# A planned kernel learns that GpSimd and VectorE exclude each other on SBUF operands

## The chip, the cores and the metric

One core of a Trainium2 chip runs the whole program. The metric is the device time of one execution in microseconds (us). A core has five engines that work side by side, each through its own instructions in a fixed order, and they meet at semaphores: TensorE (PE, matmuls), VectorE (DVE), ScalarE (ACT), GpSimd (POOL), and SyncE (SP), which issues the DMAs here. Matmuls write to PSUM; DVE and ACT read PSUM and SBUF; in this kernel POOL works on SBUF alone.

## The reference

```
# x: 8 x 8 heads x 512 x 64, state: 8 x 8 heads x 32 x 64
scores  = x @ state^T / 8 ;  xread = softmax(scores) @ state      # 512 rows a head
scores2 = state @ x^T / 8 ;  sread = softmax(scores2) @ x         # 32 rows a head
y   = concat([xread, sread]) -> (8*544) x 512
y   = ((y @ w_a) * (y @ w_b)) @ w_out                  # moe,  512 -> 1536 -> 512
out = (silu(y @ w_gate) * (y @ w_val)) @ w_out2        # moe2, 512 -> 1536 -> 512
```

The inputs x and state are fp32, the weights arrive as 64-bit floating point numbers and are converted in the kernel.

## The kernel before, in words

**Precision.** A matmul operand is held as two fp32r halves, hi and lo, and a product takes three matmuls (hi*hi, hi*lo, lo*hi). `split` and `hi_lo` (L317, L324) make the halves: ACT casts to hi, then one subtraction on DVE or POOL makes lo. There are hundreds of these subtractions; unless the source lies in PSUM, the planner may put each on DVE or on POOL (`dve_pool`).

**Weights.** `convert` (L345 to L377) turns 64-bit numbers to fp32: two ACT passes, a clamp (DVE or POOL, L363), a shift and a merge (DVE, L368 and L371), and an integer addition that only POOL does (L375). This addition occurs 72 times. `second_weights` (L689 on) makes sums and differences of converted weights on DVE (L700), splits them and sends them to DRAM.

**Attention.** `quad`, `softmax1` and `softmax2` (L479 to L632) do four heads at a time. Softmax uses 32x32 transposes and grouped reductions on DVE, an exponential on ACT, and two broadcasts (L533, L548) on DVE or POOL.

**First moe.** For each of eight blocks of 512 tokens and one of 256 state rows, `moe` (L650 to L686) multiplies by twelve weight columns a and b (L645), ACT or DVE copies a out of PSUM, DVE multiplies by b from PSUM (L664), the product is split (tile hs), and four output products (L680) add up in PSUM. Tile names ending in _s are those of the state block.

**Second moe.** `operands` and `second` (L719 to L817) handle two blocks at a time by a scheme of seven products for eight. Sums of the inputs are made on DVE (L738), fourteen splits (tile x) feed the products (L750), and DVE combines results in PSUM (L764, L771). `unit` (L844) makes the output products, `finish` (L862) adds and stores.

**The planner.** `Program` (L103 to L240) fixes the order of the work. Each call of `add` makes a task with the engines that may do it, a modelled cost on each, what it reads and writes, and a due time `by`. `order` plays a simulation of the five queues: whenever an engine is free, it takes the ready task with the earliest due time for which there is buffer room. A task that two engines may do is left for the other engine where that one would finish it sooner by the model. The outcome is an engine for each task and an order of instructions on each engine; nothing of the modelled times is enforced on the chip, where semaphores alone hold the engines. The modelled costs are L62: DVE 0.07 us and 1.05 ns a column, or 0.53 ns for fast forms, POOL 0.2 us and 2.6 ns a column. So a subtraction of 512 columns is counted as 0.61 us on DVE and 1.53 us on POOL. `HOP_US` (L64) is the modelled delay from the end of a task to the start of one that waits for it. In the model of before, DVE and POOL run independently of each other.

Of the kernel before, what the change touches and what calls it, by code (L numbers as in the profile page):

```python
# [10 lines left out]
F32 = mybir.dt.float32  # L11
# [4 lines left out]
ALU = mybir.AluOpType  # L16
AX = mybir.AxisListType

P = 128
# [40 lines left out]
ROOM = {"w": 44, "h": 20, "pt": 2}  # L60

ACT_US, DVE_US, FAST_US, POOL_US = ((0.09, 0.84e-3), (0.07, 1.05e-3), (0.07, 0.53e-3), (0.2, 2.6e-3))  # L62
PASS_US, HALF_PASS_US = 0.2267, 0.12
HOP_US, PE_HOP_US = 0.15, 0.3  # L64
DMA_US, DMA_ISSUE_US, DMA_BYTES_PER_US = 2.2, 0.5, 3.6e5

DMA_AHEAD_US = 1

# [14 lines left out]
class Buf:  # L83


    def __init__(self, tag, name, make, after=None):
        self.tag, self.name, self.make, self.after = tag, name, make, after
        self.t = None
        self.parts = {}
        self.tasks = set()  # L90


class Task:
    def __init__(self, i, engines, fn, bufs, deps, by, start, size):
# [4 lines left out]
        self.new = []  # L99
        self.engine, self.main = None, 0.0  # L100


class Program:  # L103

# [4 lines left out]
        self.tasks = []  # L109
        self.first = 0.0  # L110

    def add(self, engines, fn, r=(), w=(), by=1e9, start=0.0, size=0):
        deps, bufs = set(), []
        for x, writes in [(x, False) for x in r] + [(x, True) for x in w]:
            b, part = x if isinstance(x, tuple) else (x, None)
            assert writes or b.tasks, "read before anything wrote it"
            if writes and b.after is not None:
                deps |= b.after.tasks
            for p, (last, readers) in b.parts.items():
                if part is None or p is None or p == part:  # L120
                    if last is not None:
                        deps.add(last)
                    if writes:
                        deps |= readers
            bufs.append((b, part, writes))
        t = Task(len(self.tasks), engines, fn, list(dict.fromkeys(b for b, _, _ in bufs)), deps, by, start, size)
        t.deps.discard(t)
        for b, part, writes in bufs:
            if writes:
                if part is None:  # L130
                    b.parts = {}
                b.parts[part] = (t, set())
            else:
                for p in [p for p in b.parts if part is None or p is None or p == part]:
                    b.parts[p][1].add(t)
            b.tasks.add(t)
        self.tasks.append(t)
        return t

    def order(self):  # L140
        tasks = self.tasks
        for t in tasks:
            for d in t.deps:
                d.next.append(t)
        for t in reversed(tasks):
            for n in t.next:
                t.by = min(t.by, n.by - n.cost - HOP_US - (DMA_US + n.size / DMA_BYTES_PER_US if n.size else 0))
        room = dict(ROOM)
        left = {b: len(b.tasks) for t in tasks for b in t.bufs}
        made = set()  # L150
        waits = {t: len(t.deps) for t in tasks}
        when = dict.fromkeys(tasks, 0.0)
        gates = sorted((t for t in tasks if t.start), key=lambda t: -t.start)
        main = 0.0
        ready = {e: [] for e in ("PE", "ACT", "DVE", "POOL", "DMA")}
        free = dict.fromkeys(ready, 0.0)
        wire = 0.0
        events = []

        def offer(t):  # L160
            heapq.heappush(events, (when[t], 0, t.i, t))

        for t in tasks:
            waits[t] += t.start > 0
            if not waits[t]:
                offer(t)
        now, done = 0.0, []
        while events:
            now = events[0][0]
            main = max(main, min(now, self.first))  # L170
            while gates and gates[-1].start <= main:
                t = gates.pop()
                waits[t] -= 1
                when[t] = max(when[t], now)
                if not waits[t]:
                    offer(t)
            while events and events[0][0] <= now + 1e-9:
                _, kind, _, t = heapq.heappop(events)
                if kind == 0:
                    for e in t.engines:  # L180
                        heapq.heappush(ready[e], (t.by, t.i, t))
                elif kind == 1:
                    for b in t.bufs:
                        left[b] -= 1
                        if not left[b] and b.tag in room:
                            room[b.tag] += 1
            for e, heap in ready.items():
                if free[e] > now + 1e-9:
                    continue
                held = []  # L190
                while heap:
                    item = heapq.heappop(heap)
                    t = item[2]
                    if t.engine is not None:
                        continue
                    t.new = [b for b in t.bufs if b not in made]
                    need = {}
                    for b in t.new:
                        if b.tag in room:
                            need[b.tag] = need.get(b.tag, 0) + 1  # L200
                    if any(room[k] < n + (RESERVE[k] if t.by > main + FAR_US else 0) for k, n in need.items()) or any(
                        max(free[o], now) + sum(q[2].engines[o] for q in ready[o] if q < item and q[2].engine is None)
                        + c < now + t.engines[e] - (SPARE_US if e != "DVE" and t.by > main + 5 else 0) - 1e-9
                        for o, c in t.engines.items() if o != e
                    ):
                        held.append(item)
                        continue
                    for k, n in need.items():
                        room[k] -= n
                    made.update(t.new)  # L210
                    t.engine, t.at = e, now
                    us = t.engines[e] * (2.0 if e == "PE" and t.engines[e] < 1.0 and main <= self.first else 1.0)
                    free[e] = end = now + us
                    main = max(main, t.main)
                    if e == "DMA":
                        wire = max(wire, now) + t.size / DMA_BYTES_PER_US
                        end = max(wire, end) + DMA_US
                        free[e] = max(free[e], wire - DMA_AHEAD_US)
                    heapq.heappush(events, (free[e], 2, t.i, t))
                    heapq.heappush(events, (end, 1, t.i, t))  # L220
                    for n in t.next:
                        waits[n] -= 1
                        hop = HOP_US if e != "PE" else 0.0 if "PE" in n.engines else PE_HOP_US
                        when[n] = max(when[n], end + hop)
                        if not waits[n]:
                            offer(n)
                    done.append(t)
                    break
                for item in held:
                    heapq.heappush(heap, item)  # L230
        self.end = now
        assert len(done) == len(tasks), f"{len(tasks) - len(done)} tasks found no room, at {now:.0f} us"
        return done
# [8 lines left out]
class Kernel:  # L242
# [32 lines left out]
    def bank(self, name, out=None):  # L275

        if out is not None:
            return self.ring(f"po{out}", 1, name, self.ps)
        return Buf("pt", name, lambda: self.ps.tile([P, 512], F32, tag="pt", bufs=ROOM["pt"], name=name))

    def dram(self, name, shape, dtype=F32):
        return Buf(None, name, lambda: self.dr.tile(shape, dtype, tag=name, name=name))
# [1 line left out]
    def ring(self, tag, n, name, pool=None, dtype=F32, shape=(512,)):  # L284

        old = self.rings.setdefault(tag, [])
        pool = pool or self.sb
        b = Buf(
            None, name, lambda: pool.tile([P, *shape], dtype, tag=tag, bufs=n, name=name),
            old[-n] if len(old) >= n else None,  # L290
        )
        old.append(b)
        return b

# [226 lines left out]
    def softmax1(self, b, g, sT, by):  # L521
# [3 lines left out]
        sn = self.h_buf(f"sn{nm}")  # L525
        mx, sm = (self.ring(k, 2, f"{k}{nm}", shape=(16, 1)) for k in ("mx", "sm"))
        grouped = lambda t: t.rearrange("p (a n) -> p a n", n=NS)
        kw = {"by": by}
        self.vec(512, lambda v: v.transpose(sn.t, sT.t), [sT], [sn], **kw)
        self.vec(  # L530
            512, lambda v: v.tensor_reduce(mx.t[:, :, 0], grouped(sn.t), axis=AX.X, op=ALU.max), [sn], [mx], **kw
        )
        self.p.add(dve_pool(512), lambda e: self.by_engine[e].tensor_tensor(  # L533
            out=grouped(sn.t), in0=grouped(sn.t), in1=mx.t.to_broadcast([P, 16, NS]), op=ALU.subtract
# [2 lines left out]
            act(512), lambda e: nc.scalar.activation(out=sn.t, in_=sn.t, func=AF.Exp, scale=SCALE), [], [sn], **kw  # L537
        )
        self.vec(
            512, lambda v: v.tensor_reduce(sm.t[:, :, 0], grouped(sn.t), axis=AX.X, op=ALU.add), [sn], [sm], **kw  # L540
        )

        def rest(v):
# [5 lines left out]
            out=grouped(sn.t), in0=grouped(sn.t), in1=sm.t.to_broadcast([P, 16, NS]), op=ALU.mult  # L549
        ), [sm], [sn], **kw)  # L550
        at = self.h_buf(f"at{nm}")
        self.vec(512, lambda v: v.transpose(at.t, sn.t), [sn], [at], **kw)
        return self.split(f"xs{nm}", at, **kw)

    def softmax2(self, b, g, sT, split, by):
# [5 lines left out]
        kw = {"by": by}  # L561
# [2 lines left out]
            v.tensor_reduce(st.t[:, 0:1], sT.t, axis=AX.X, op=ALU.max)  # L564
            v.tensor_scalar(out=st.t[:, 1:2], in0=st.t[:, 0:1], scalar1=-SCALE, scalar2=None, op0=ALU.mult)

        self.vec(620, first, [sT], [st], start=by - 35, **kw)
        self.p.add(act(512), lambda e: nc.scalar.activation(
            out=e2.t, in_=sT.t, func=AF.Exp, scale=SCALE, bias=st.t[:, 1:2], accum_out=st.t[:, 2:3]
        ), [sT], [e2, st], **kw)  # L570
# [478 lines left out]
```

## Time and profile before

| | |
|---|---|
| median of 3 runs | 1563.6 us (1561.76 to 1568.19) |
| profiled execution | 1562.1 us, of which the span of the trace is 1560.3 us |
| PE busy | 1482.2 us (95%) |
| DVE busy | 1109.7 us (71%) |
| ACT busy | 675.9 us (43%) |
| POOL busy | 360.3 us (23%), 256 instructions |

Time outside the span of the profiled execution is 1.8 us. A busy share is the union of the instructions' spans on an engine. The wait views name, for an idle stretch of an engine, the instruction whose semaphore ended it. In lists of groups, buffer numbers are left out of tile names, and a line can be a helper's, so that L317 stands for every subtraction made by `split` and `hi_lo`. PEclk is the granted TensorE clock as a share of 2.4 GHz, so 0.5 is 1.2 GHz.

### The profile page before, as it was taken

To read this page: it belongs to the slowest core of one execution; us is meant where nothing else is said; L and a number is where in the kernel's file an instruction comes from. 1 tells how busy PE (TensorE), PEld (TensorE's weight loads), DVE (VectorE), ACT (ScalarE), POOL (GpSimd) and SP (SyncE) were. 2 spreads that over 40 slices of the span, in tenths; PEclk is the share of its full clock that TensorE was granted. 3 is DMA by queue.
4 is the path that set the end of the run, shared out by engine and by line. 5 is a ranking of instruction groups with operands and counts; after the bars stand their busy time and mean duration, and the time that the engine had idled before them with its cause. 6 is when DMAs were issued, how large, how long until landed. Compare 5 with 4: busy or idle time off the path is not lost.

```text
span 1560.3 us, 19362 instructions
## 1 busy us (share of the span) xinstructions
PE 1482.2 (95%) x6792; PEld 1218.3 (78%) x6792; DVE 1109.7 (71%) x1676; ACT 675.9 (43%) x1196; POOL 360.3 (23%) x256
## 2 busy tenths in 40 slices
PE   4798899899999999999999989999999999999998
PEld 1577687688887888898777778888788887888887
DVE  8999767866789898776686896555855568545554
ACT  6676655653556576554442432221413123222220
POOL 3525212421234343333321340000200021000000
PEclk9899999899999999999999999999999999999999
DMA  7665564563455555656875668646464555622411
GB/s 285 211 236 197 177 220 145 176 205 122 152 189 206 202 205 216 230 203 216 334 259 200 238 236 305 220 157 221 167 231 168 189 202 173 218 95 108 162 68 68
DMA packets 111185, 304.84 MB, mean 195 GB/s; under 512 B 11760, under 2 KB 13808, under 8 KB 111088
## 3 DMA queue, kind: packets, MB, share of 16 engines
q1 hardware_dynamic: 111088, 303.61, 54.8%
q8 instruction: 53, 0.87, 0.2%
q14 instruction: 44, 0.36, 0.1%
HBM read 222.30 MB, written 80.74 MB: 194 GB/s over the span
## 4 chain that ended last, share of the span: by engine, by line
PE 52%; DVE 8%; issue 2%; DMA 1%; ACT 1%; POOL 1%; SPq 0%; DVEq 0%; POOLq 0%; ACTq 0%
PE pu L844 15%; PE pC L750 7%; PE pB L750 7%; PE pA L750 7%; PE pD L750 3%; PE po L680 3%; PE p L645 3%; PE p_s L645 2%; DVE s L738 1%; PE pvs L645 1%; PE pgs L645 1%; PE pus L844 1%; DVE x L317 1%; PE po_s L680 1%; DVE t L764 1%
## 5 line engine op out<-in xcount | busy, mean ns | idle before, releaser
L680 PE MATMUL po<-hs,wo 128*128 128x512 f32 x1152 | 289.7, 395 | 2.6 <-ACT hs L324 1.5
L645 PE MATMUL p<-xs,swh 128*128 128x512 f32 x768 | 243.4, 398 | 15.0 <-ACT xs L324 5.5
L680 PEld LDWEIGHTS po<-hs,wo 128*128 128x128 f32 x1152 | 218.3, 191 | 48.6 <-ACT hs L324 1.9
L645 PEld LDWEIGHTS p<-xs,swh 128*128 128x128 f32 x768 | 144.7, 191 | 50.2 <-DVE a L664 6.5
L645 PE MATMUL p<-xs,swl 128*128 128x512 f32 x384 | 151.8, 395 | 1.2 <-DVE swl L317 1.1
L750 PE MATMUL pB<-x,w 128*128 128x512 f32 x576 | 146.6, 390 | 2.0 <-DVE t L764 2.0
L750 PE MATMUL pA<-x,wg 128*128 128x512 f32 x576 | 148.0, 393 | 0.0
L844 PE MATMUL pu<-wo,hv 128*128 128x512 f32 x576 | 140.6, 389 | 0.0
L844 PE MATMUL pu<-wo,hu 128*128 128x512 f32 x576 | 138.6, 389 | 0.0
L750 PEld LDWEIGHTS pB<-x,w 128*128 128x128 f32 x576 | 108.2, 188 | 25.4 <-DVE t L764 2.8
L750 PEld LDWEIGHTS pA<-x,wg 128*128 128x128 f32 x576 | 109.5, 190 | 23.1
L844 PEld LDWEIGHTS pu<-wo,hu 128*128 128x128 f32 x576 | 107.9, 188 | 22.2
L844 PEld LDWEIGHTS pu<-wo,hv 128*128 128x128 f32 x576 | 107.9, 188 | 22.2
L768 ACT ACTIVATE av<-t 128x512 f32<-128x512 f32 x48 | 30.4, 632 | 211.2 <-DVE t L764 211.1
L317 POOL TENSOR_TENSOR hv<-av,hv 128x512 fp32r<-128x512 f32 x21 | 33.8, 1610 | 379.9 <-ACT hv L324 346.6
L764 DVE TENSOR_TENSOR t<-c,pB 128x512 f32<-128x512 f32 x96 | 65.6, 683 | 72.0 <-PE pB L750 71.7
L317 POOL TENSOR_TENSOR hs<-a,hs 128x512 fp32r<-128x512 f32 x40 | 62.5, 1562 | 179.1 <-ACT hs L324 169.6
L664 DVE TENSOR_TENSOR a<-a,p 128x512 f32<-128x512 f32 x96 | 65.5, 682 | 50.4 <-PE p L645 48.5
L324 ACT CAST hs<-a 128x512 fp32r<-128x512 f32 x96 | 59.6, 621 | 69.3 <-DVE a L664 56.2
L645 PEld LDWEIGHTS p<-xs,swl 128*128 128x128 f32 x384 | 73.3, 191 | 17.6 <-DVE swl L317 2.0
L750 PE MATMUL pC<-x,wv 128*128 128x512 f32 x288 | 75.3, 398 | 9.9 <-DVE c L764 9.9
L862 DVE TENSOR_TENSOR part<-part,pu 128x512 f32<-128x512 f32 x64 | 43.8, 684 | 51.1 <-PE pu L844 51.1
(205 smaller groups left out, 2682.1 us busy)
## 6 DMA issues: line engine op xcount, KB each, us to landing
w<-w SPq DMA_DIRECT2D x120, 512.0 KB, 5.3
sw<-swo SPq DMA_DIRECT2D x96, 256.0 KB, 2.5
wg<-w2g SPq DMA_DIRECT2D x48, 512.0 KB, 4.7
wv<-w2v SPq DMA_DIRECT2D x48, 512.0 KB, 5.0
wo<-w2o SPq DMA_DIRECT2D x48, 512.0 KB, 5.6
swr<-sw SPq DMA_DIRECT2D x47, 512.0 KB, 5.1
raw_w<-in_wab SPq DMA_DIRECT2D x24, 512.0 KB, 6.5
xt<-in_xt SPq DMA_DIRECT2D x32, 256.0 KB, 5.5
```

The costliest lines, as they stand in the source:

```text
L317: lambda e: self.by_engine[e].tensor_tensor(out=out(), in0=in0(), in1=in1(), op=ALU.subtract), r, w, **kw
L324: self.p.add(act(n), lambda e: self.nc.scalar.copy(hi(), src()), [src_buf], [hb], **kw)
L645: pe.matmul(ps.t[:, :n], lhsT=l, rhs=r, start=i == 0, stop=i == last)
L664: self.vec(n, lambda v, a=a, pb=pb: v.tensor_tensor(out=a.t[:, :n], in0=a.t[:, :n], in1=pb.t[:, :n], op=ALU.mult), [pb], [a])
L680: pe.matmul(ps.t[:, :n], lhsT=wo[f].t[:, hw, c], rhs=hs.t[:, hh, :n], start=st, stop=sp)
L738: self.vec(512, lambda e, o=o, a=a, b=b, op=op: e.tensor_tensor(out=o.t, in0=a.t, in1=b.t, op=op), [a, b], [o])
L750: pe.matmul(ps.t, lhsT=w.t[:, hw, c], rhs=x.t[:, hx], start=start and i == n == 0, stop=stop and i == 1 and n == 2, skip_group_check=True)
L764: self.vec(512, lambda e: e.tensor_tensor(out=out.t, in0=ta(), in1=tb(), op=op), [a, b], [out])
L768: p.add(act(n), lambda e: nc.scalar.activation(out=a.t[:, :n], in_=g.t[:, :n], func=AF.Sigmoid), [g], [a])
L844: pe.matmul(ps.t, lhsT=h.t[:, hh, c], rhs=wo[f].t[:, hw], start=f == steps[0] and i == 0, stop=f == steps[-1] and i == 2)
L862: self.vec(w, lambda v: v.tensor_tensor(out=to(), in0=part.t[:, j % 2, :w], in1=ps.t[:, :w], op=ALU.add), [ps, (part, j)], [ok], by=by)
```

## The change

Only the planner's model is touched. A task gets a flag `port`, which says that it works on SBUF operands alone; a task that touches a PSUM tile has it false, and the transposes and reductions of softmax are set to false by hand. In the simulation, a POOL task or a DVE task with the flag occupies a shared resource until its modelled end; until then neither POOL nor a DVE task with the flag may start. DVE tasks without the flag are free to. Besides, a task that both DVE and POOL may do goes to POOL only when the DVE tasks without the flag that are ready and waiting add up to at least `BESIDE_US`, 0.9 us. The POOL additions of `convert` have no other engine and are exempt from this. `HOP_US` rises from 0.15 to 0.25. What is computed stays the same.

```diff
-HOP_US, PE_HOP_US = 0.15, 0.3
+HOP_US, PE_HOP_US = 0.25, 0.3
+BESIDE_US = 0.9
 class Buf:
+        self.psum = False                     # bank() and rings in PSUM set it to True
 class Task:
+        self.port = False
 def add(...):
-    def add(self, engines, fn, r=(), w=(), by=1e9, start=0.0, size=0):
+    def add(self, engines, fn, r=(), w=(), by=1e9, start=0.0, size=0, port=None):
+        t.port = not any(b.psum for b in t.bufs) if port is None else port
 def order(self):
+        shared = 0.0
...
                 held = []
+                blocked = shared > now + 1e-9 and e in ("DVE", "POOL")
                 while heap:
...
+                    if blocked and (e == "POOL" or t.port):
+                        held.append(item)
+                        continue
+                    if e == "POOL" and "DVE" in t.engines and sum(
+                        q[2].engines["DVE"] for q in ready["DVE"] if q[2].engine is None and not q[2].port
+                    ) < BESIDE_US:
+                        held.append(item)
+                        continue
...
                     free[e] = end = now + us
+                    if e == "POOL" or e == "DVE" and t.port:
+                        shared = end
# softmax1: both transposes and both reductions; softmax2: the first reduction
-        self.vec(512, lambda v: v.transpose(sn.t, sT.t), [sT], [sn], **kw)
+        self.vec(512, lambda v: v.transpose(sn.t, sT.t), [sT], [sn], port=False, **kw)
```

## Rows read from the trace of the kernel before

**Rows 1.** The page's first part: busy us (share of span) and instructions, by engine.
```profile
PE 1482.2 (95%) x6792; PEld 1218.3 (78%) x6792; DVE 1109.7 (71%) x1676; ACT 675.9 (43%) x1196; POOL 360.3 (23%) x256
```

**Rows 2.** Busy us by engine in stretches, then PEclk, DMA share, GB/s.
```profile
36.00:160.00 124.00, 105.22 (x428) 80.36 (x428) 120.30 (x186) 89.64 (x165) 53.44 (x41) 0.96 0.62 215
160.00:300.00 140.00, 129.12 (x566) 103.69 (x567) 103.21 (x161) 81.65 (x146) 38.88 (x26) 0.95 0.50 171
...
300.00:560.00 260.00, 257.04 (x1162) 211.65 (x1161) 201.38 (x311) 148.52 (x253) 82.36 (x56) 1.00 0.55 190
560.00:640.00 80.00, 75.05 (x358) 63.17 (x357) 68.70 (x112) 50.82 (x100) 27.11 (x18) 0.96 0.53 192
640.00:800.00 160.00, 154.30 (x860) 134.56 (x859) 113.90 (x162) 79.30 (x142) 55.12 (x38) 0.98 0.70 258
800.00:960.00 160.00, 152.09 (x654) 124.01 (x653) 125.63 (x183) 57.20 (x97) 37.65 (x26) 0.98 0.67 240
960.00:1555.80 595.80, 592.77 (x2745) 494.89 (x2743) 347.61 (x522) 144.43 (x257) 53.30 (x38) 1.00 0.47 166
```

**Rows 3.** Waits of PE: what it waited for, us in total, times, longest.
```profile
PE pC L750 <- DVE c L764: 9.9, 7, 4.5
...
PE p L645 <- ACT xs L324: 5.5, 1, 5.5
...
PE sw L431 <- DVE a L311: 4.3, 1, 4.3
...
PE psr L605 <- DVE a L317: 3.8, 1, 3.8
```

**Rows 4.** The stretch around one of these waits, in order of time: start, us.
```profile
917.09 2.99 POOL L317 TENSOR_TENSOR x<-x2l,x 128x512 fp32r<-128x512 f32 x2 [1.86 <-ACT x L324]
917.13 1.80 DVE L738 TENSOR_TENSOR s<-x2l,x2l 128x512 f32<-128x512 f32 x1
...
925.72 0.68 DVE L764 TENSOR_TENSOR t<-c,pB 128x512 f32<-128x512 f32 x1
...
926.32 0.68 DVE L738 TENSOR_TENSOR s<-x2l,x2l 128x512 f32<-128x512 f32 x1
```

**Rows 5.** Groups of DVE by form: count, busy us, mean ns, idle before.
```profile
L764 DVE TENSOR_TENSOR t<-c,pB 128x512 f32<-128x512 f32 x96 | 65.6, 683 | 72.0 <-PE pB L750 71.7
L317 DVE TENSOR_TENSOR hs<-a,hs 128x512 fp32r<-128x512 f32 x56 | 47.3, 844 | 16.4 <-ACT hs L324 16.1
L317 DVE TENSOR_TENSOR w<-cv_w,w 64x512 fp32r<-64x512 f32 x48 | 42.8, 892 | 1.3
L371 DVE SCALAR_TENSOR_TENSOR cv_w<-raw_w,cv_w 128x512 uint32<-128x512 uint32 x24 | 25.2, 1074 | 0.1
L738 DVE TENSOR_TENSOR s<-x2l,x2l 128x512 f32<-128x512 f32 x16 | 15.9, 1006 | 0.0
```

**Rows 6.** Busy us and count of POOL's L317, then of its L375.
```profile
0.00:1561.00 1561.00, 230.20 (x152) 0.98 0.55 195
0.00:1561.00 1561.00, 104.28 (x72) 0.98 0.55 195
```

**Rows 7.** Order of time: a POOL addition that begins just behind a DVE subtraction.
```profile
159.82 0.69 DVE L317 TENSOR_TENSOR w<-cv_w,w 64x512 fp32r<-64x512 f32 x1
159.87 1.77 POOL L375 TENSOR_TENSOR cv_wo<-cv_wo 128x512 int32<-128x512 int32 x1 [2.07 <-DVE cv_wo L371]
160.43 1.28 DVE L311 COPY a<-pa 128x512 f32<-128x512 f32 x2
```

**Rows 8.** Groups on POOL in 36 to 160: its additions there.
```profile
L375 POOL TENSOR_TENSOR cv_w<-cv_w 128x512 int32<-128x512 int32 x12 | 18.6, 1562 | 9.4 <-DVE cv_w L371 9.4
...
L375 POOL TENSOR_TENSOR cv_wo<-cv_wo 128x512 int32<-128x512 int32 x5 | 7.9, 1580 | 10.3 <-DVE cv_wo L371 5.3 <-ACT cv_wo L357 5.0
```

**Rows 9.** Stretches of 1.2 GHz behind two of the long waits, columns as in rows 2.
```profile
56.00:66.40 10.40, 6.33 (x14) 4.58 (x15) 10.09 (x12) 6.46 (x12) 4.56 (x3) 0.51 0.54 164
...
926.40:933.40 7.00, 5.75 (x14) 4.53 (x15) 5.13 (x9) 1.96 (x4) 3.65 (x3) 0.51 0.00 1
```

More of the change, by code (lines that the diff above doesn't have):

```diff
@@ L278, in bank @@
             return self.ring(f"po{out}", 1, name, self.ps)
-        return Buf("pt", name, lambda: self.ps.tile([P, 512], F32, tag="pt", bufs=ROOM["pt"], name=name))
+        b = Buf("pt", name, lambda: self.ps.tile([P, 512], F32, tag="pt", bufs=ROOM["pt"], name=name))
+        b.psum = True
+        return b
     def dram(self, name, shape, dtype=F32):
@@ L291, in ring @@
         )
+        b.psum = pool is self.ps
         old.append(b)
@@ L528, in softmax1 @@
         kw = {"by": by}
-        self.vec(512, lambda v: v.transpose(sn.t, sT.t), [sT], [sn], **kw)
+        self.vec(512, lambda v: v.transpose(sn.t, sT.t), [sT], [sn], port=False, **kw)
         self.vec(
-            512, lambda v: v.tensor_reduce(mx.t[:, :, 0], grouped(sn.t), axis=AX.X, op=ALU.max), [sn], [mx], **kw
+            512, lambda v: v.tensor_reduce(mx.t[:, :, 0], grouped(sn.t), axis=AX.X, op=ALU.max), [sn], [mx], port=False, **kw
         )
@@ L539, in softmax1 @@
         self.vec(
-            512, lambda v: v.tensor_reduce(sm.t[:, :, 0], grouped(sn.t), axis=AX.X, op=ALU.add), [sn], [sm], **kw
+            512, lambda v: v.tensor_reduce(sm.t[:, :, 0], grouped(sn.t), axis=AX.X, op=ALU.add), [sn], [sm], port=False, **kw
         )
@@ L551, in softmax1 @@
         at = self.h_buf(f"at{nm}")
-        self.vec(512, lambda v: v.transpose(at.t, sn.t), [sn], [at], **kw)
+        self.vec(512, lambda v: v.transpose(at.t, sn.t), [sn], [at], port=False, **kw)
         return self.split(f"xs{nm}", at, **kw)
@@ L565, in first @@
             v.tensor_scalar(out=st.t[:, 1:2], in0=st.t[:, 0:1], scalar1=-SCALE, scalar2=None, op0=ALU.mult)
-        self.vec(620, first, [sT], [st], start=by - 35, **kw)
+        self.vec(620, first, [sT], [st], start=by - 35, port=False, **kw)
         self.p.add(act(512), lambda e: nc.scalar.activation(
```

## Prediction

> **What bounds the kernel now.** The first view to read is the page's first part. PE is busy 1482.2 of 1560.3 us [rows 1], so only 78 us of the span are open to a change of order, and the engine that PE waits for is to be found. The table by stretch comes next [rows 2]. In its rows the reader subtracts PE's busy time from the length: 18.8 us idle in 36 to 160, 10.9 in 160 to 300, 3.0 in 300 to 560, 4.9 in 560 to 640, 5.7 in 640 to 800, 7.9 in 800 to 960 and 3.0 from there to the last matmul. These are 54 us. The other 24 lie ahead of 36 us and behind the last matmul, where first loads, conversions and the last store set the pace; I leave them as they are.
>
> The column of the granted clock belongs to it: 0.96, 0.95, 0.96, 0.98 and 0.98 in five of the seven rows. A mean of 0.96 over 124 us is 5.0 us of full-speed work that was not done; the five rows make 5.0 + 7.0 + 3.2 + 3.2 + 3.2 = 21.6. Two rows show when the clock is low: from 56.0 to 66.4 and from 926.4 to 933.4 it is 0.51, near the lower level of 1.2 GHz, and each begins in or behind a long idle time of PE [rows 9]. Idle time inside such a row counts in both sums (4.1 us of the first row, at half clock 2), so I take 18 for the clock. Stalls and their clock are 72 us.
>
> The waits of PE say who ended them [rows 3]. The longest single ones, 4.5, 5.5, 4.3 and 3.8 us, are ended by DVE, or by an ACT cast of a tile that DVE's softmax made. So the question is why DVE was late, although it is busy only 71%.
>
> The stretch in front of one of them shows it [rows 4]. POOL begins a subtraction at 917.09; at 917.13 DVE begins an operation on two SBUF inputs and takes 1.80 us; the same operation at 926.32 takes 0.68. The grouped view of DVE confirms it over the run [rows 5]. The operation with one input in PSUM has a mean of 683 ns over 96 instructions, but forms with both inputs in SBUF have 844, 892, 1074 and 1006. The reverse is there too: a POOL addition that begins 0.05 us behind a DVE subtraction takes 1.77 us, and two copies from PSUM pass beside it in 1.28 us, 0.64 each [rows 7]. What the planner is about to learn is thus what the trace shows.
>
> **The change part by part.** *Which work moves.* POOL has 256 instructions [rows 1]. 72 are the additions that have no other engine, 152 are subtractions of L317 [rows 6], and some 26 of the other 32 are broadcasts and clamps that DVE may do. So 178 can move. They stay on POOL only where DVE tasks without the flag, worth 0.9 us, wait in the queue. DVE's PSUM work mostly waits for PE instead of queueing (72.0 us of idle time before one group of L764 [rows 5]), so I take 25 that stay, between 0 and 100. 153 move.
>
> *What they cost on DVE.* The DVE instructions at 925.72 and 926.32 follow each other at 0.60 us, though each span is 0.68 [rows 4]. 153 x 0.60 = 92 us more DVE work. ACT's cast in front of each subtraction is unchanged, and the moved work issues nothing to a DMA queue.
>
> *What is relieved.* Against 683 ns the four forms lost 56 x 161 + 48 x 209 + 24 x 391 + 16 x 323 ns = 9.0 + 10.0 + 9.4 + 5.2 = 33.6 us [rows 5]. They are 144 of 1676 DVE instructions, and other SBUF forms can lose as well. The lower bound for the whole is 34; the upper one, if each of some 250 POOL instructions held one DVE operation by 1.80 - 0.68 = 1.1 us, is 275. I take 100, nearer to the low end, since that end was read from rows; it is 0.4 us for each POOL instruction. The 72 additions stay and keep their share, 72 x 0.4 = 29. So 71 us go.
>
> *The sum on DVE* is 92 - 71 = +21 us on 1110. The gain can't come from less work; it can only come from order. In the row pair at 917, POOL's two subtractions cost DVE 1.1 us at the first [rows 4]; as DVE's own work both would cost 1.2. If moved splits stay in front of the operation that PE waits for, nothing comes back (bound 0 of the 72 us, and below nothing as the rival on the slower side has it). If they go behind it, all of it does (bound 72). The planner takes the earliest due time first, and a split that a later product reads is due later; the old model did not know that DVE would be late, the new one does. Both ends are equally near to the rows, and I take the half: 36.
>
> *What the exclusion costs.* In the new plan a DVE task with the flag may not start beside an addition. That hurts where DVE is full: 120.3 of 124 us in 36 to 160 [rows 2], with 12 + 5 = 17 additions [rows 8]. The model counts an addition as 1.33 us and a DVE task of 512 columns as 0.61, so beside an addition up to 0.72 us of DVE stay empty: 17 x 0.72 = 12 us, and nothing where PSUM work is ready to fill it. I take the 12, on the path, because DVE has 3.7 us to spare there. The hop of 0.25 for 0.15 moves due times by 0.1 us a link, about 1 us over ten links; on the chip it costs nothing by itself, and I take 0 between -2 and +2.
>
> *The sum.* -36 + 12 = -24 us against the profiled execution of 1562.1 (span 1560.3 and 1.8 around it): 1538. The median of the runs shown is 1.5 above that execution, so the forecast is 1539.5.
>
> A rule of the Trainium skill speaks against the plan. The page SBUF — State Buffer, section Who interferes with whom, says that the order of issue, not the form of the operation, decides which engine is held up. The trace agrees: with POOL first, DVE took 1.80 us; with DVE first, POOL took 1.77 [rows 4, 7]. By the rule, additions that stay on POOL hold DVE operations in an order that no plan fixes, as the first rival has it.
>
> **The rivals.** *No change, 1562 (chance 0.17).* A modelled exclusion is no semaphore: the remaining additions start when their inputs are there. If each holds a DVE operation by 1.1 us, 79 us of delay stay, and of the 100 only 21 go. Then DVE runs behind the new plan as it ran behind the old one, and the recovery shrinks to the 12 us that the exclusion costs: 1562.1, within 8. For it speaks that DVE's sum doesn't fall; against it that the splits on POOL are twice as many as the additions [rows 6]. That 100 of the 178 stay on POOL, so that the change hardly does what it says, would end here too.
>
> *Slower, 1579 (0.16).* DVE becomes the bound in 36 to 160. POOL has 41 instructions there [rows 2], 24 of them movable: 24 x 0.60 = 14 us, and 12 of planned emptiness, against 3.7 to spare and 24 x 0.4 = 10 relieved. DVE is 13 us late, PE waits for it, and the clock adds 4 (half of a 7 us row at 0.51 [rows 9]): 1562.1 + 17 = 1579. It decides from the point at which what is added to DVE there exceeds 14 us. Against it: ACT is busy only 89.6 of the 124 us [rows 2] and can take copies out of PSUM that DVE does now.
>
> *Everything comes back, 1510 (0.15).* The plan, now true to the chip, keeps the evictions on time: 72 less 12, less some 8 for stalls without POOL in them, is 52 us. For it speaks 300 to 560, where PE idles 3.0 of 260 us though POOL is busy for 82 [rows 2]: there the order is right already. Against it: 18.8 of the 54 us idle lie where DVE is full.
>
> **How the numbers follow.** The forecast, with 0.52, spans recoveries from 0.3 to 0.7 of the 72 us: 1525 to 1554 on the scale of the median. The range, 1510 to 1573, leaves out about half of the full recovery and two thirds of the slower case. A measurement of this kernel can tell about 0.5%, 8 us, from no change. Faster: 0.52, less 0.02 at its edge, and 0.15 make 0.65. Same: 0.17 and that edge, 0.19. Slower: 0.16.
>
> **What would show it.** Right: POOL falls from 256 to about 100 instructions and from 360 to about 140 us; the means of L317 on DVE come down towards 690 ns; DVE's total stays within 40 us of 1110; the idle time of PE that I subtracted from the stretches shrinks from 54 to about 30 us, and PEclk is 1.00 in most of them behind 160. Wrong: new PE waits of over 3 us in 36 to 160 with DVE full (the slower rival); means of L371 and L738 on DVE still near 1000 ns, held by the additions (no change); or a PE idle sum between 36 us and the last matmul that stays over 45.

## The result

The changed kernel takes 1516.0 us (median of 4 runs, 1515.7 to 1518.5) against 1563.0 before: a ratio of 0.970, 95% interval 0.968 to 0.971, 47 us less. The forecast was 24 us less, to 1539.5. The time lies inside the range, the sign was right, and the size was off by a factor of two.

The first part of the page answers to [rows 1].

```profile
PE 1464.8 (97%) x6792; PEld 1207.6 (80%) x6792; DVE 1111.3 (73%) x1834; ACT 675.0 (45%) x1202; POOL 120.4 (8%) x92
```

POOL went from 256 instructions to 92: 72 additions, six that set up constants, and 14 others. DVE has 158 instructions more and the same busy time, 1111.3 for 1109.7. So DVE, the engine that PE waits for, has no less to do, as the prediction had it. The table by stretch answers to [rows 2]; the last column but two is the granted clock.

```profile
36.00:160.00 124.00, 106.78 (x428) 79.03 (x426) 113.06 (x190) 83.24 (x151) 29.57 (x20) 0.93 0.54 190
160.00:300.00 140.00, 131.74 (x599) 105.20 (x599) 113.94 (x183) 92.79 (x170) 25.04 (x18) 1.00 0.57 199
300.00:560.00 260.00, 259.59 (x1182) 215.36 (x1183) 209.27 (x353) 155.13 (x272) 25.98 (x19) 1.00 0.55 194
560.00:640.00 80.00, 80.00 (x449) 70.08 (x449) 72.35 (x134) 53.30 (x107) 10.81 (x8) 1.00 0.60 219
640.00:800.00 160.00, 160.00 (x845) 138.54 (x844) 115.50 (x197) 74.81 (x130) 12.14 (x9) 1.00 0.71 261
800.00:960.00 160.00, 160.00 (x707) 132.38 (x706) 126.63 (x207) 56.62 (x96) 9.86 (x7) 1.00 0.75 273
960.00:1509.90 549.90, 549.86 (x2561) 460.91 (x2559) 331.24 (x529) 133.48 (x237) 0.00 (x0) 1.00 0.45 160
```

Subtracted as before, PE idles 17.2 + 8.3 + 0.4 + 0 + 0 + 0 + 0.04 = 25.9 us from 36 us to the last matmul, where it had been 54.2. Behind 300 us nothing is left: 24.6 us had been there. The clock is at 1.00 in every row but the first, whose 0.93 is 8.7 us of work not done, against 21.6 over the five rows of before. Ahead of 36 us the granted clock of this execution is 0.72 where it had been 1.00, with as many matmuls done by then, 29 for 28. Idle time gave 28 us and the clock up to 13. The last matmul ends at 1509.9 instead of 1555.8, 46 us earlier; the other 5 lie within the time in which PE counts as busy, and the views do not show what they are.

The groups of DVE answer to [rows 5]; lines have moved by 21.

```profile
L338 DVE TENSOR_TENSOR hs<-a,hs 128x512 fp32r<-128x512 f32 x93 | 67.2, 725 | 12.7 <-ACT hs L345 11.5
L785 DVE TENSOR_TENSOR t<-c,pB 128x512 f32<-128x512 f32 x96 | 65.8, 686 | 81.7 <-PE pB L771 80.5 <-ACT hu L345 0.9
...
L338 DVE TENSOR_TENSOR w<-cv_w,w 64x512 fp32r<-64x512 f32 x48 | 37.6, 783 | 2.4 <-ACT w L422 1.1
...
L392 DVE SCALAR_TENSOR_TENSOR cv_w<-raw_w,cv_w 128x512 uint32<-128x512 uint32 x24 | 22.3, 958 | 0.1
...
L759 DVE TENSOR_TENSOR s<-x2l,x2l 128x512 f32<-128x512 f32 x16 | 10.8, 686 | 0.3 <-DMA x2l<-x 0.2
...
L392 DVE SCALAR_TENSOR_TENSOR cv_v<-raw_v,cv_v 128x512 uint32<-128x512 uint32 x12 | 8.5, 704 | 0.1
...
L392 DVE SCALAR_TENSOR_TENSOR cv_o<-raw_o,cv_o 128x512 uint32<-128x512 uint32 x12 | 8.4, 703 | 0.1
```

The sums s of the second moe came down from 1006 to 686 ns: they have no POOL work beside them any more. The group cv_w, made right in front of POOL's additions, only fell from 1074 to 958. What is left of the exclusion comes from the additions: with them cut short (`after_tiny_add` below) cv_w has 686. The longest wait of PE in the changed kernel shows it, in order of time:

```profile
51.94 0.42 DVE L389 TENSOR_SCALAR cv_w<-cv_w 128x512 uint32<-128x512 uint32 x1
...
52.60 4.66 DVE L392 SCALAR_TENSOR_TENSOR cv_w<-raw_w,cv_w 128x512 uint32<-128x512 uint32 x4
...
53.37 6.42 POOL L396 TENSOR_TENSOR cv_w<-cv_w 128x512 int32<-128x512 int32 x4 [6.21 <-DVE cv_w L392]
...
57.18 1.48 DVE L389 TENSOR_SCALAR cv_wo<-cv_wo 128x512 uint32<-128x512 uint32 x1
58.59 1.75 DVE L338 TENSOR_TENSOR hs<-a,hs 128x512 fp32r<-128x512 f32 x1
...
60.86 2.35 DVE L338 TENSOR_TENSOR xts<-xt,xts 128x512 fp32r<-128x512 f32 x2
61.02 1.64 POOL L396 TENSOR_TENSOR cv_wo<-cv_wo 128x512 int32<-128x512 int32 x1 [1.23 <-DVE cv_wo L392]
...
63.13 0.48 DVE L338 TENSOR_TENSOR stt<-strt,stt 128x128 fp32r<-128x128 f32 x2
...
63.47 0.79 PE L515 MATMUL psc<-xts,stt 128*128 128x512 f32 x1 [7.76 <-DVE stt L338]
```

Four merges take 4.66 us on DVE, where four at the pace of 0.60 [rows 4] make 2.4, with POOL's additions beside them; a shift, which has one SBUF input, takes 1.48 for 0.42; two subtractions take 2.35 instead of 1.2; PE stands for 7.76 us behind them. In the plan's model these operations do not meet; on the chip the additions start when their inputs are there.

### The profile page after: what moved, and what is told of

The parts are those of the page before. It is cut to its first block, busy times and chain, and to the rows that moved or that the text cites. A ratio compares the mean times of both kernels' runs of the same rounds, so it can differ in the third digit from the quotient of the medians.

```text
span 1514.3 us, 19283 instructions
## 1 busy us (share of the span) xinstructions
PE 1464.8 (97%) x6792; PEld 1207.6 (80%) x6792; DVE 1111.3 (73%) x1834; ACT 675.0 (45%) x1202; POOL 120.4 (8%) x92
## 4 chain that ended last, share of the span: by engine, by line
PE 88%; DVE 6%; ACT 3%; DMA 1%; issue 1%; SPq 0%; DVEq 0%; ACTq 0%
PE pu L865 17%; PE po L701 15%; PE p L666 14%; PE pC L771 9%; PE pA L771 9%; PE pB L771 9%; PE pD L771 4%; PE p_s L666 2%; PE psr L626 1%; DVE w L338 1%; PE pvs L666 1%; PE po_s L701 1%; PE pgs L666 1%; PE sw L452 1%; PE pus L865 1%
## 5 line engine op out<-in xcount | busy, mean ns | idle before, releaser
L701 PE MATMUL po<-hs,wo 128*128 128x512 f32 x1152 | 284.6, 391 | 3.9 <-DVE hs L338 2.8
L701 PEld LDWEIGHTS po<-hs,wo 128*128 128x128 f32 x1152 | 214.7, 188 | 50.1 <-DVE hs L338 3.7
L666 PE MATMUL p<-xs,swh 128*128 128x512 f32 x768 | 239.4, 393 | 2.5 <-DVE a L685 2.5
L330 ACT COPY a<-p 128x512 f32<-128x512 f32 x86 | 50.4, 586 | 80.4 <-PE p L666 75.0
L338 DVE TENSOR_TENSOR hs<-a,hs 128x512 fp32r<-128x512 f32 x93 | 67.2, 725 | 12.7 <-ACT hs L345 11.5
```

The source lines that it names most:

```text
L330: self.nc.scalar.copy(out(), in_())
L338: lambda e: self.by_engine[e].tensor_tensor(out=out(), in0=in0(), in1=in1(), op=ALU.subtract), r, w, **kw
L666: pe.matmul(ps.t[:, :n], lhsT=l, rhs=r, start=i == 0, stop=i == last)
L701: pe.matmul(ps.t[:, :n], lhsT=wo[f].t[:, hw, c], rhs=hs.t[:, hh, :n], start=st, stop=sp)
```

## The experiments

All were timed in three rounds or more against the kernel before on the same chip; ratios to it are given with their 95% interval. The quotes are what was put down ahead of each run: theory A says that the gain needs a plan that knows the exclusion, rival B that fewer POOL tasks are enough.

### What holds DVE: POOL's reading, or the length of its tasks

`before_memset` keeps the order of the kernel before and puts a memset in the place of each subtraction on POOL.

```diff
-lambda e: self.by_engine[e].tensor_tensor(out=out(), in0=in0(), in1=in1(), op=ALU.subtract)  # ...
+lambda e: self.nc.gpsimd.memset(out().bitcast(F32), 0.0) if e == "POOL" else
+    self.by_engine[e].tensor_tensor(out=out(), in0=in0(), in1=in1(), op=ALU.subtract)  # ...
```

> The kernel before, with its order and its engines, but each subtraction that it gives to POOL is replaced by a memset of the same tile to zero; the subtraction is left out, so the low halves made there are zeros. POOL then writes and does not read. If DVE's delays come from POOL's reading beside it (what both theories hold), only the 72 additions and some 26 others still hold DVE: the DVE group hs falls from 844 to about 720 ns and the time to 1500 to 1530. If POOL's tasks delay PE by their own length of 1.5 us and not through DVE, the time falls as well, but the DVE groups cv_w L371 and w L317 keep their means; if neither, 1550 to 1565.

Measured: 1514.9 us, ratio 0.969 (0.968 to 0.971). But a memset is also shorter, 0.53 us, so `before_memset3` gives POOL its length back.

```diff
+lambda e: [self.nc.gpsimd.memset(out().bitcast(F32), 0.0) for _ in range(3)] if e == "POOL" else  # ...
```

> As before_memset, but three memsets for each subtraction, so that POOL is busy about 1.6 us in place of 0.53 and still reads nothing; the subtraction is left out. If the gain of before_memset (1514.9) came from DVE no longer being held, the time stays within 15 us of it, 1505 to 1530, with the DVE group hs near 750 ns. If it came from the low halves being ready sooner, the time goes back towards the kernel before: 1545 to 1565.

Measured: 1515.6 us, ratio 0.969 (0.967 to 0.970). Its page, first part, and two groups of DVE:

```profile
PE 1462.4 (97%) x6792; PEld 1207.3 (80%) x6792; DVE 1039.1 (69%) x1676; ACT 674.8 (45%) x1196; POOL 354.2 (23%) x560
```

```profile
L372 DVE SCALAR_TENSOR_TENSOR cv_w<-raw_w,cv_w 128x512 uint32<-128x512 uint32 x24 | 21.0, 899 | 0.1
L739 DVE TENSOR_TENSOR s<-x2l,x2l 128x512 f32<-128x512 f32 x16 | 10.7, 685 | 0.0
```

POOL is as busy as before, 354 us for 360: its 152 subtractions took 230 us, the 456 memsets take 228. DVE loses 71 us of busy time: the sums s run in 685 ns, 9 of these 16 beside a memset, while cv_w beside the additions, which read, still has 899. POOL's length alone costs nothing that shows. One thing was not separated by a run: a memset need not wait for ACT's cast, so the low halves are there earlier too. In the waits of PE before, none is ended by POOL, which speaks against this as the cause.

### Moving the work without planning it

`blind_move` takes the order of before and issues on DVE, at their places, the 178 tasks that were POOL's.

```diff
-            t.fn(t.engine)
+            t.fn("DVE" if t.engine == "POOL" and "DVE" in t.engines else t.engine)
```

> The order of the kernel before, planned without the exclusion, but each of the 178 tasks that the plan gives to POOL and that DVE may do is issued on DVE at its place in the plan. Theory A (the gain needs a plan that knows the exclusion): DVE carries about 100 us of work that its plan did not count, PE's waits keep their size in other places, 1545 to 1580. Rival B (fewer POOL tasks are enough, whatever the plan knows): within 10 us of the changed kernel, 1506 to 1526.

Measured: 1550.1 us, ratio 0.992 (0.990 to 0.993), inside A's interval. Four of the waits of PE; the second and the last answer to rows of [rows 3]:

```profile
PE sw L431 <- DVE swo L311: 5.5, 3, 2.8
PE pC L750 <- DVE c L764: 5.4, 7, 2.7
PE sw L432 <- DVE st_lo L317: 4.8, 2, 3.5
PE sw L431 <- DVE a L311: 3.7, 1, 3.7
```

The sums s are at 681 ns here too, but DVE has its moved subtractions in front of what PE waits for. The wait for c on L750 went from 9.9 to 5.4 us, that for a on L431 from 4.3 to 3.7. In sizes: without the subtractions' hold and without their work on DVE the kernel is 48 us faster (the memsets); their work on DVE, in an order that did not count it, gives 35 back; and the whole change is 34 faster than that. These are differences of the same four times, and do not test each other.

### The three parts of the change, one by one and in pairs

Six variants complete the set of hop, 0.9 us rule and exclusion. Two are the changed kernel without the exclusion, and without the rule:

```diff
-                blocked = shared > now + 1e-9 and e in ("DVE", "POOL")
+                blocked = False                                          # no_lock
```

> The changed kernel without the exclusion in the plan: the 0.9 us rule and the hop of 0.25 stay, so that the plan puts about 30 movable tasks on POOL. Theory A: the plan counts on DVE beside the 72 additions, which DVE does not get; part of PE's waits come back, 1530 to 1550. Rival B: 1506 to 1526, as the changed kernel.

```diff
-BESIDE_US = 0.9
+BESIDE_US = 0.0                                                          # no_beside
```

> The changed kernel with BESIDE_US at 0: the plan knows the exclusion, but 138 movable tasks stay on POOL instead of 14. Theory A in its strong form (knowledge is what counts): within 10 us of the changed kernel, 1506 to 1530. Rival B (the number of POOL tasks counts): 1540 to 1565, with forms on two SBUF inputs near 900 ns on DVE.

The hop alone, put into the kernel before, and the changed kernel with the hop of before:

```diff
-HOP_US, PE_HOP_US = 0.15, 0.3
+HOP_US, PE_HOP_US = 0.25, 0.3                                            # hop_only
```

> The kernel before with HOP_US at 0.25 and nothing else. Both theories: no effect of its own, 1555 to 1570. A rival, that a good part of the gain is the truer hop: under 1550.

```diff
-HOP_US, PE_HOP_US = 0.25, 0.3
+HOP_US, PE_HOP_US = 0.15, 0.3                                            # after_hop15
```

> The changed kernel with HOP_US back at 0.15. If the hop does nothing by itself: 1508 to 1526, within 10 us of the changed kernel to either side. If it carries a part of the gain: over 1526.

The rule alone is `no_lock`, and the exclusion alone is `no_beside`, both with this hop of 0.15:

> The kernel before with the 0.9 us rule alone: no exclusion in the plan, hop 0.15. If fewer tasks on POOL, planned as such, carry most of the gain: 1518 to 1530. If hop and rule are both needed for the 1521.5 of the variant without exclusion: 1530 to 1550.

> The kernel before with the exclusion in the plan alone: no 0.9 us rule, hop 0.15; 147 movable tasks stay on POOL. If knowledge alone does two thirds, as with the hop (1531.2): 1528 to 1545. If the hop carried most of that: 1545 to 1562.

| parts in the plan | us | ratio (95%) |
|---|---|---|
| hop (`hop_only`) | 1542.4 | 0.986 (0.984 to 0.987) |
| rule (`beside_only`) | 1523.6 | 0.975 (0.973 to 0.977) |
| exclusion (`lock_only`) | 1519.7 | 0.972 (0.970 to 0.974) |
| hop, rule (`no_lock`) | 1521.5 | 0.974 (0.972 to 0.976) |
| hop, exclusion (`no_beside`) | 1531.2 | 0.980 (0.978 to 0.981) |
| rule, exclusion (`after_hop15`) | 1520.6 | 0.972 (0.970 to 0.974) |
| all (the change) | 1516.0 | 0.970 (0.968 to 0.971) |

Neither A nor B stands as put: A missed `no_lock`, and `no_beside` came out between the two, 1 us above A's interval. `lock_only` was faster than either of its expectations. Rule or exclusion alone brings 40 or 44 of the 47 us, so they cure largely the same thing, one by taking work off POOL, the other by ordering it. The exclusion alone leaves POOL busy for 273 us and the sums s at 860 ns, and PE is still hardly idle behind 300 us:

```profile
300.00:560.00 260.00, 259.15 (x1178) 214.21 (x1177) 204.63 (x336) 153.65 (x269) 54.25 (x40) 1.00 0.55 192
560.00:960.00 400.00, 398.39 (x1990) 339.46 (x1991) 308.57 (x495) 184.58 (x333) 91.41 (x64) 1.00 0.72 259
```

How long DVE is held can be estimated from single instructions: for each one that ran beside POOL, its time above that of the same operation without POOL. The sum is 115 us before, 35 in the changed kernel, 66 in `lock_only` and 34 in `blind_move`. So the length of the hold alone does not decide: with the exclusion planned DVE is held twice as long as in the blind move and is busy 33 us less, and the kernel is 30 us faster.

The hop was expected to do nothing and brought 22 us alone. Added to the exclusion it costs 11, added to both it brings 5. Two more kernels, the one before with hops of 0.14 and 0.35, asked whether that is size or luck.

```diff
-HOP_US, PE_HOP_US = 0.15, 0.3
+HOP_US, PE_HOP_US = 0.14, 0.3                                            # hop14; 0.35: hop35
```

> The kernel before with HOP_US at 0.14 in place of 0.15, a change of no meaning that shuffles the order all the same. It tells how far any reshuffling moves the time. If hop_only's 1542.4 is mostly the luck of another order: this one differs from the 1564 of before by 10 us or more, to either side. If the size of the hop did it: 1558 to 1570.

> The kernel before with HOP_US at 0.35. If a longer hop makes the plan truer, because it leaves room for the delays that the plan doesn't know: 1525 to 1545, at or under hop_only's 1542.4. If hop_only was luck: anywhere from 1545 to 1575.

Measured: 1568.1 us for 0.14, ratio 1.003 (1.001 to 1.004), and 1548.1 for 0.35, 0.989 (0.987 to 0.992), 3 us outside the interval expected of a true effect. The one reshuffling without meaning that was tried moves the time by 4 us; both longer hops gain 16 to 22. But the same hop of 0.25 costs 11 us beside the exclusion, so differences of some 5 us between two plans can be order alone. With the hop of 0.25 DVE is held as before:

```profile
L317 DVE TENSOR_TENSOR hs<-a,hs 128x512 fp32r<-128x512 f32 x72 | 60.0, 834 | 21.9 <-ACT hs L324 21.6
...
L738 DVE TENSOR_TENSOR s<-x2l,x2l 128x512 f32<-128x512 f32 x16 | 16.2, 1024 | 2.5 <-DMA x2l<-x 2.5
```

The means of 834 and 1024 stand against 844 and 1006. A longer hop may leave room that absorbs the delays; that it does so was not shown.

### What the additions cost, before and after

`one_sided` takes away the planned emptiness of DVE beside an addition.

```diff
-                    if blocked and (e == "POOL" or t.port):
+                    if blocked and e == "POOL":
```

> The changed kernel, but in the plan only POOL waits for DVE's SBUF tasks; DVE may start such a task while POOL is busy. This takes away the emptiness that the plan leaves on DVE beside the 72 additions. If that emptiness costs 12 us, as the prediction had it: 1500 to 1510. If it costs nothing, or DVE's half of the exclusion is what makes the plan true: 1514 to 1526, up to the 1521.5 of the variant without any exclusion.

Measured: 1521.4 us, ratio 0.973 (0.971 to 0.975). The emptiness does not cost 12 us; without it the kernel is 5 slower, which can be order alone. In 36 to 160 DVE is full again, 120.7 us for 113.1 in the changed kernel, and PE idles as long, 16.7 us for 17.2:

```profile
36.00:160.00 124.00, 107.29 (x437) 80.86 (x438) 120.65 (x207) 90.44 (x166) 30.92 (x23) 0.93 0.59 205
```

What the additions do on the chip is told by cutting them to 8 of 512 columns, in the order of the changed kernel and in that of before:

```diff
-nc.gpsimd.tensor_tensor(out=t.t[:, 0].bitcast(I32), in0=t.t[:, 0].bitcast(I32), ...
+nc.gpsimd.tensor_tensor(out=t.t[:, 0, :8].bitcast(I32), in0=t.t[:, 0, :8].bitcast(I32), ...
```

> The changed kernel with its order and engines, but each of the 72 additions on POOL does 8 of its 512 columns; the other 504 are left out, so the converted weights miss what the addition brings. What the additions still cost by holding DVE goes away. The prediction left 29 us of DVE delay to them: if that is on the path in 36 to 300 us, 1500 to 1511. If the plan has put it where DVE has time: 1512 to 1518. Slower than 1520 would say that an addition that ends early upsets the order.

> The kernel before, with its order and engines, but each of the 72 additions on POOL does 8 of its 512 columns; the other 504 are left out. The prediction added 12 us for the additions as a new cost of the exclusion. If the kernel before paid for them already, by DVE operations held behind them, it loses about as much as the changed kernel did (13 us): 1545 to 1556, and the 12 us were counted twice. If the cost is new: 1558 to 1566.

Measured: 1503.2 us in the new order, ratio 0.961 (0.959 to 0.964), and 1527.7 in the old one, 0.977 (0.975 to 0.979). The full additions cost 13 us after the change and 36 before it. The expectation of 1545 to 1556 for the old order was missed on the far side: they were dearer there than anyone had put them. The hold of DVE is not all that a cut addition takes away: it lasts 0.34 us for 1.45, so its weight is ready sooner, and ACT's waits ended by POOL fall from 29.6 to 8.1 us in the old order. The two were not separated. In the new order cv_w now has its own time; in the old order cut additions leave PE idle 10.3 us in 36 to 160, where it had been 18.8.

```profile
L392 DVE SCALAR_TENSOR_TENSOR cv_w<-raw_w,cv_w 128x512 uint32<-128x512 uint32 x24 | 15.8, 686 | 0.1
```

```profile
36.00:160.00 124.00, 113.66 (x469) 87.03 (x470) 120.44 (x197) 96.38 (x177) 36.49 (x42) 0.97 0.65 224
```

Without the last movable tasks on POOL:

```diff
-BESIDE_US = 0.9
+BESIDE_US = 1e9                                                          # never_pool
```

> The changed kernel with BESIDE_US so high that no task that DVE may do goes to POOL: 73 planned POOL tasks in place of 89. If the last movable tasks on POOL still hold DVE to any effect: 1508 to 1515. If they are well placed, or it is too few to see: 1514 to 1524.

Measured: 1514.6 us, ratio 0.969 (0.967 to 0.971), no difference to the change that can be told.

### Going on: no addition on POOL

`or_merge` is the changed kernel with the low bits cut off instead of rounded, so that an OR can merge them on DVE.

```diff
-out=t.t[:, 0], in0=t.t[:, 0], scalar1=3, scalar2=None, op0=ALU.logical_shift_left    # tensor_scalar
+out=t.t[:, 0], in0=t.t[:, 0], scalar=3, in1=t.t[:, 1],
+op0=ALU.logical_shift_left, op1=ALU.bitwise_or                                       # scalar_tensor_tensor
...
-self.p.add({"POOL": POOL_US[1] * 512}, lambda e: nc.gpsimd.tensor_tensor(... op=ALU.add), [(t, 1)], [hi], **kw)
# ACT's pass over the low word gets bias=-0.4999
```

> A way to go on: the changed kernel without the 72 additions on POOL. The low bits are cut off instead of rounded and merged by an OR that takes the place of DVE's shift, so that POOL has 24 tasks in the plan. after_tiny_add showed 13 us to be had (1503.2). DVE's shift of 0.36 to 0.42 us becomes a form on two inputs of 0.60 to 0.69, 72 x 0.25 = 18 us of work, most of it where DVE has time. If the lock by the additions is the bound: 1500 to 1510. If DVE's longer work takes its place in 36 to 300 us: 1512 to 1525.

Measured: 1495.7 us, ratio 0.957 (0.955 to 0.959): 20 us under the changed kernel, under both expectations, and the fastest of all. Its first part and two of its groups:

```profile
PE 1458.0 (98%) x6792; PEld 1208.8 (81%) x6792; DVE 1094.8 (73%) x1835; ACT 676.2 (45%) x1197; POOL 19.6 (1%) x24
```

```profile
L338 DVE TENSOR_TENSOR hs<-a,hs 128x512 fp32r<-128x512 f32 x91 | 62.1, 683 | 10.8 <-ACT hs L345 10.1
...
L393 DVE SCALAR_TENSOR_TENSOR cv_w<-raw_w,cv_w 128x512 uint32<-128x512 uint32 x24 | 15.6, 681 | 0.1
```

Forms on two SBUF inputs run close to 683 ns now, and DVE's busy time fell by 16 us although 72 shifts became longer forms.

## Why the prediction was right, and where its sizes failed

**What was right.** What bounds the kernel was read correctly: PE's stalls come from DVE, DVE's lateness from operations on two SBUF inputs that find POOL reading, and the clock takes a second toll [rows 2, 4, 5, 9]. POOL came out at 92 instructions and 120 us for the forecast 100 and 140; DVE's total stayed, as the sum of +21 us implied within its 40; PE's idle time fell to 25.9 us for the forecast 30; the clock is 1.00 behind 160. That work moved without a plan brings little is shown by `blind_move`. One wait was passed over: the second longest of PE, 4.6 us up to 37 us, is ended by ACT's cast st_hi, and with memsets on POOL it is still there, 5.0 us, so it isn't the subtractions' doing.

**The step that failed: the recovery.** A half of 72 us was taken for the whole kernel, 36, between ends said to be equally near. By the same measure up to 41 came back, 28 of idle time and up to 13 of clock, and 46 by the end of the last matmul. No part of the run shows a half. From 36 to 300 us, 8 of 42 came back: idle time fell from 29.7 to 25.5 us, and what the clock takes from 12.0 to 8.7. Behind 300 us all 34 came back: idle time fell from 24.6 to 0.4 us, the clock's part from 9.6 to 0.

How full DVE is does not tell the stretches apart: 560 to 640, with DVE busy 72 of 80 us, recovered all of its 4.9, while 160 to 300, with 114 of 140, kept 8.3 of its 10.9. What tells them apart is where DVE is still held. The merges cv_w all begin ahead of 300 us and stay at 958 ns; those of the later weights, cv_v and cv_o, came from 800 to 704 and 703. By the estimate from single instructions the hold went from 31 to 23 us in 36 to 300, and from 80 to 11 behind. The prediction had the hold nearly right, 100 us with 29 that stay, for 115 and 35. It did not ask where the 29 would lie. Most of them lie in 36 to 300, where little came back; behind that all of the stalls could go, where it took a half. Ahead of 300 us `after_tiny_add` ties the two together: with the additions cut, PE idles 12.1 us for 17.2 in 36 to 160, and 2.8 for 8.3 in 160 to 300.

**What the exclusion costs.** The prediction added 12 us, "up to 0.72 us of DVE stay empty" beside each of 17 additions [rows 8], "on the path". For 36 to 160 its sum thus comes near what was measured: half of 24 us less 12 is nothing, and nothing came back there, idle time 1.6 us down and the clock's part 3.7 up. That is luck. The emptiness came, DVE is busy 113.1 us there for 120.3, and it was not on PE's path: `one_sided` fills it, and PE idles 16.7 us for 17.2. The additions' hold keeps a part of the stalls there. That hold isn't new: full additions cost 36 us in the old order by `before_tiny_add` and 13 in the new one, though these two contain weights that are ready sooner, and parts of this kind overlap and don't add up. The sum counted the additions' hold as staying (29 us of DVE time) and then charged for them once more.

**The hop.** It was put at 0 between -2 and +2. Alone it is worth 22 us. A constant of the model that costs nothing on the chip still changes the order, and the prediction had no row for what an order is worth.

**The rivals.** No change and slower did not come. DVE's 36 to 160 did keep its stalls, as the slower rival said, but not by moved work: `after_tiny_add` has PE idle 12.1 us there instead of 17.2, so the additions are a part of it. The full recovery, 1510, had a chance of 0.15 and came nearest.

```profile
36.00:160.00 124.00, 111.95 (x459) 84.15 (x456) 108.78 (x202) 90.69 (x163) 16.16 (x22) 0.96 0.61 208
160.00:300.00 140.00, 137.24 (x633) 111.72 (x632) 109.75 (x192) 97.10 (x178) 6.58 (x19) 1.00 0.63 213
```

What stays open: why a longer hop helps the old order and hurts the exclusion alone, and what the other 12 us of idle time in 36 to 160 are made of; without any addition, in `or_merge`, 8.2 of them are left.

## What to carry to other kernels

An engine that holds up another should be charged for what it delays there. Here 256 POOL instructions looked like free help at 23% busy, and removing the reads of 152 of them while keeping their time was worth 3%. Ask also where in the run the rest of the delay will lie, and not only how much of it stays. When a term is added for a cost that stays after a change, look first whether the kernel before pays it already: cut the suspect to a few columns in both orders. And a planner's constants should be tried one at a time, with meaningless variations as the yardstick; the one tried here gave 0.3%, and one is few.

## What the runs showed of the hardware

POOL's memsets do not hold DVE's operations on two SBUF inputs: 228 us of memsets left the sums s at 685 ns, where 230 us of subtractions had made it 1006. The Trainium skill, page SBUF — State Buffer, section Who interferes with whom, says that an operation with two SBUF inputs contends with a GpSimd instruction that reads SBUF and not with one that only writes; the trace agrees, 1006 against 685 ns. The group with one input in PSUM [rows 5] has 683 before and 686 after; before, the 21 of its 96 that ran beside POOL took 681 ns in the mean, the others 684. Two inputs are not needed to be held: the shift with one SBUF input took 1.48 us beside the additions, 0.42 without. And the fastest kernel adds to the plan that nearly nothing is left on POOL: without the additions the forms come to 681 to 683 ns and the kernel to 1495.7 us.
